# Attention with local band and global keys, then Fourier mixing and a two-layer block: global keys in small blocks of the array, and rows 4 and 5 read backwards

## The chip, the cores and the metric

The kernel runs on one core of a Trainium2 chip. A core has five engines with a queue each: TensorE (PE, matrix products out of SBUF into PSUM banks), VectorE (DVE), ScalarE (ACT), GpSimd (POOL, which here issues most loads) and SyncE (SP, which issues transfers). An engine runs its own queue in order; semaphores tie the queues together. The metric is the device time of one execution in microseconds (us), median over runs.

TensorE multiplies a stationary operand that has been loaded into its array (the weights) with a moving one that is streamed through. The array can be used whole, written 128\*128 (rows \* columns), or as smaller blocks such as 64\*64, 64\*128 or 128\*32, each with its own weights. The rows are the contracted side, the columns the partitions of the result. A `tile_position` names the corner of the block.

## What is computed

Four batches, eight heads, 768 positions, head size 64. Attention in which a query sees the 96 keys up to itself and the first eight keys of the sequence ("global" ones), with a bias by distance; for a global key outside the band the distance counts as 96.

```python
scores = scale * np.matmul(q, k.transpose(0, 1, 3, 2))
is_global = pos[None, :] < int(n_global)                 # 8
is_local = (rel >= 0) & (rel < int(n_local))             # 96
dist = np.where(is_global & ~is_local, float(n_local), np.abs(rel))
scores = scores - slopes[:, None, None] * dist
scores = np.where(is_global | is_local, scores, -1e9)
a = softmax(scores);  x = a @ v          # then heads side by side: x is (4, 768, 512)
mixed = np.real(fft(fft(x, axis=1), axis=2))
u = x + mixed
un = (u - mean(u)) / np.sqrt(var(u) + 1e-06)
out = u + np.maximum(un @ w_ch1, 0.0) @ w_ch2            # 512 -> 2048 -> 512
```

The mixed part has a symmetry: with x real, row s and column n of it equal row 768 - s and column 512 - n (both taken modulo their length).

## The kernel before

The whole kernel is one stream of instructions. Functions name units of work with their needs and costs, and a planner (`Plan`) walks through them with its own clock for each engine, and emits whichever can start first. Its costs, and small numbers in a table `BIAS` that favour or delay single units, set the order; nothing is decided while the kernel runs. There are four streams of TensorE units: MIX (Fourier mixing), ATT (attention), PH (first product of the two-layer block) and PG (second product).

**Attention**, by batch `b` and pair of heads `hp`. `load_qk` and `load_v` bring q, k and v in, through POOL's queue; only the first pair's q and k come as 32-bit through SP (L426) and are cast by an engine (L443). `trans` transposes q and k on TensorE (L507), or, from batch 2, a transfer does it (L485). `score` makes local scores: 64\*64 blocks in batches 0 and 1 (L549 adds the bias as a product, L559), 64\*128 blocks later (L555); ScalarE's exponential follows (L583 or L580). A 128-row block of queries has two blocks of keys, its own and the one before.

Global keys have a path of their own. `kg_copies` puts each head's eight global keys into a 32-column tile `kG`, in which every head has its own eight columns and the others hold zeros. `glob` makes scores of four heads at a time in a 128\*32 block (L639): the two products of a half add up, since each fills only its heads' rows. `v_global` gathers the eight heads' global values by a selecting product (L606) into `vG`, 64 rows (eight per head) by head; in the columns of head h all rows but h's eight are zero. A column of ones, made once by `ones` (L1423), gives the softmax its denominator. One exponential makes `EG` (L652).

`av` multiplies: for each of six blocks of queries it adds, in one place of a PSUM bank, the local products of both heads (L685, 65 columns: 64 values and the ones) and, from the third block on, one product of `EG` with both heads' part of `vG`, 130 columns (L677). Both use the whole array. VectorE divides by the denominator (L702, L704).

**Mixing.** In batches 1 to 3 `bounce` writes x to memory and reads it back with six sequence positions a partition (`XD`, `XR`), all through ScalarE's queue (L725, L732). `fold_s` and `fold_d` (VectorE) and `y_unit` (L914) make a transform of which only half is computed; the rest is the same data mirrored. `mirror` makes reversed copies on POOL: `r0` for rows 0 and 3 (L949 to L951), `rn` for the others (L962). `u_unit` makes u for a pair of rows (positions 6m + r) in one PSUM bank: the pairs are (1, 2), (0, 3), (4, 5), 16 products of 128 columns each (L1017). In batch 0 x is added into the bank by permuting products in 64\*64 blocks (L993, `spread`), in the others VectorE adds `XR` (L1039). Then comes the centring (L1073 and L1075), a transpose (`nt_unit`, L1114) and the sum of squares (L1082), with POOL's power (L1089, L1090).

**Two-layer block.** `ph_unit` (L1144) makes hidden units, ScalarE or VectorE applies the threshold (L1150, L1151), `pg_unit` (L1168) multiplies with the second weights, VectorE scales and adds u (L1177), SP stores (L1182). The last four of the twelve pairs of rows use a form with fewer products (L1249).

The planner charges 0.1 us where a unit marked narrow follows one that is not; the units of `av` are not marked.

Of the kernel before, what the change touches and what calls it, by code (L numbers as in the profile page):

```python
# [22 lines left out]
class Plan:  # L23
# [11 lines left out]
    def __init__(self):  # L35
        self.t = {"PE": 0.0, "ACT": 0.0, "DVE": 0.0, "POOL": 0.0, "SP": 0.7, "DMA": 3.75, "DMA2": 1.9}
        self.tok = {}
        self.ready = []
        self.pending = []
        self.rings = {}  # L40
        self.left = {}
        self.n = 0
        self.lanes = [0.0] * 8
        self.soft = [0.0] * 8
# [64 lines left out]
    def emit(self, place):  # L109
# [8 lines left out]
        if dma:  # L118
            q = "DMA2" if outs and outs[0] in (("ld", 0), ("ld", 1), ("c", "id"), ("c", "dist"), ("c", "gb")) else "DMA"
# [29 lines left out]
    def slot(self, tag):  # L149
# [7 lines left out]
    BIAS = {('mk1', '*', 4): 1.5, ('y', 1, 2, 2, 'r'): -3, ('qk', '*', 2): -0.7, (2, 90): -0.7, ('ob', '*', 2): -0.3,  # L157
            (3, '*', 7): -1.5, ('ex', 2, 2, 0): 1.5, ('ss', '*', 6): 0.3, (0, 20): -3, (1, 57): -0.7, ('mk1', '*', 5): 1.5,
            ('v', '*', 1): 1.5, ('c', 't2'): -0.3, ('mk1', '*', 7): 0.7, ('kG', '*', 1): 0.7, ('z', 1, 0): 3, ('u', 2, 0): 0.7}
# [4 lines left out]
    AQ = (4, 5)  # L164
    ORD = {("qk", 0): 0, ("v", 0): 0, ("qk", 1): 5, "w1": 6, "gate": 7, ("v", 1): 8, "w2": 9, ("qk", 2): 10, ("v", 2): 10, ("qk", 3): 10, ("v", 3): 10}
# [42 lines left out]
def act(n):  # L208
    return 0.06 + n / 1200.0


def dve(n):
    return 0.085 + n / 960.0
# [11 lines left out]
def kernel(  # L225
# [63 lines left out]
    sel = np.zeros((P, 128))  # L289
    gpos = np.flatnonzero(tau < NG)  # L290
    for h in range(4):
        for g in range(NG):
            sel[gpos[g], h * 32 + h * NG + g] = 1.0
    gb = np.zeros((64, 1))
    for h in range(H):
        at = 32 * (h // 2 % 2) + 16 * (h // 4) + 8 * (h % 2)
        gb[at:at + NG, 0] = -slopes[h] * NL
    perm = np.zeros((P, 9, 64))
    for rho in range(3):
        for jj in range(3):  # L300
            for m in range(64):
                y = 3 * m + rho - 64 * jj
                if 0 <= y < 64:
                    perm[y, 3 * rho + jj, m] = perm[64 + y, 3 * rho + jj, m] = 1.0
    ident_sel = np.concatenate([np.eye(P), sel], 1)
# [45 lines left out]
    ident = kon.tile([P, 256], FP16, tag="ident", name="ident")  # L351
    sel_sb = ident[:, 128:256]
# [4 lines left out]
    gb_sb = kon.tile([64, 1], FP32, tag="gb", name="gb")  # L357
# [7 lines left out]
    one = kon.tile([P, 1], FP16, tag="one", name="one")  # L365
# [3 lines left out]
    vG = [kon.tile([P, H, 66], FP16, tag=f"vG{i}", name=f"vG{i}") for i in range(2)]  # L369

    EG = kon.tile([P, 512], FP16, tag="eg", name="eg")
# [32 lines left out]
    def load_qk(b, hp):  # L404
# [3 lines left out]
        for w, src in enumerate((q, k)):  # L408
# [14 lines left out]
            if n == 0:  # L423
                def read(w=w, rows=rows):
                    t = stage["u", w] = buf("u", w, [P, 2 * NP, 2 * Dh], FP32, 1)
                    nc.sync.dma_start(t, rows)  # L426
                pl.later([("SP", 0.45, read)], [], 0.0, [("ld", w)], lat=1.7, dma=1.35)

                def cast(on, w=w):
                    place()  # L430
                    copy_on(on, qk16[n][:, w].rearrange("p h n t d -> p (h n) (t d)"), stage["u", w])
                pl.later([("ACT", act(768), lambda cast=cast: cast("ACT")), ("DVE", dve(768), lambda cast=cast: cast("DVE"))], [("ld", w)], 0.0,
                         [("qk", 0, w)], [("free", "u", w)], rank=0)
# [34 lines left out]
    def kg_copies(b, hp):  # L468
        n = HP * b + hp
        for s in range(2):  # L470
            def cp(on, s=s):
                c0 = 16 * (hp // 2) + 8 * s
                on.tensor_copy(  # L473
                    kG[b % 2][64 * s:64 * s + 64, hp, c0:c0 + NG].rearrange("p (t m) -> p t m", t=2),
                    TT[n][64 * s:64 * s + 64, 1, 0:P].rearrange("p (t m) -> p t m", t=2)[:, :, 0:NG // 2])
# [1083 lines left out]
```

## Time and profile before

The median of three runs is 263.35 us (262.07 to 263.92). The profiled execution took 262.43 us, its span from the first to the last instruction is 260.5 us. Durations are from that execution.

| what | instructions | busy us | mean ns of one |
|---|---|---|---|
| ph, first product (L1144) | 768 | 93.3 | 273 |
| pg, second product (L1168) | 256 | 61.1 | 379 |
| local attention products (L685) | 352 | 16.9 | 193 |
| global attention products (L677) | 64 | 12.6 | 220 |
| mixing, u (L1017), from plain tiles | 112 | 8.5 | 219 |
| adding x in batch 0 (L993) | 36 | 4.6 | 622 |
| global scores (L639) | 16 | 3.4 | 383 |
| reversed copies on POOL (L962) | 16 | 10.1 | 661 |
| VectorE's add of x to u (L1039) | 18 | 11.7 | 688 |
| exponential of global scores (L652) | 5 | 3.4 | 677 |

A row of the profile names the line, the engine, what is written and read, and the size as partitions x elements. Matmuls overlap, so their lengths add up to more than the busy time, and the price of one in a stream is the distance from its start to that of the next.

### The profile page before, as it was taken

How to read it: one execution, taken by the hardware profiler on the slowest of the kernel's cores; microseconds unless marked ns; L12 is line 12 of the kernel's file. 1: busy time of each engine (PE TensorE's matmuls, PEld its weight loads, DVE VectorE, ACT ScalarE, POOL GpSimd, SP SyncE). 2: the span in 40 equal slices, each digit the busy share in tenths (PEclk: the TensorE clock that was granted, in tenths of full speed). 3: DMA queues.
4: the chain of work that ended last, by engine and by line, in shares of the span. 5: the costliest groups of instructions: out<-in, count | busy, mean ns of one | idle time of the engine just before them, and what ended most of it. 6: DMA issues, size and time to landing. Idle time of an engine off the chain costs nothing.

```text
span 260.5 us, 6774 instructions
## 1 busy us (share of the span) xinstructions
PE 246.3 (95%) x2824; PEld 178.8 (69%) x2824; DVE 163.1 (63%) x362; ACT 142.9 (55%) x240; POOL 120.6 (46%) x212
## 2 busy tenths in 40 slices
PE   7798789899979999999999999999999999999994
PEld 2566545589748676575477466588779578888883
DVE  1549996537982746712277987778996555625463
ACT  4198798685636698851055743884645236533300
POOL 8798876724938988999921304030304011010000
PEclk9799999999999999999999999999999999999999
DMA  7999999997999999999968941401450540300222
GB/s 175 174 165 179 274 207 108 90 194 102 138 159 218 158 138 149 140 112 123 114 126 167 178 182 48 115 3 43 108 178 0 83 121 0 93 30 3 81 83 81
DMA packets 93630, 31.52 MB, mean 121 GB/s; under 512 B 81664, under 2 KB 89984, under 8 KB 93600
## 3 DMA queue, kind: packets, MB, share of 16 engines
q0 software_dynamic: 66096, 14.18, 62.5%
q1 hardware_dynamic: 24672, 12.19, 21.2%
q10 hardware_dynamic: 2832, 4.72, 6.9%
q8 instruction: 22, 0.36, 0.6%
q14 instruction: 8, 0.07, 0.1%
HBM read 30.95 MB, written 8.65 MB: 152 GB/s over the span
## 4 chain that ended last, share of the span: by engine, by line
PE 55%; POOL 19%; DMA 17%; ACT 3%; DVE 3%; issue 2%; ACTq 0%; POOLq 0%
PE ph L1144 18%; PE pg L1168 12%; POOL qk L414 10%; DMA v<-in_v_dram 7%; DMA qk<-in_q_dram 6%; PE pgD L1249 5%; POOL v L400 5%; DMA w<-in_moe_w_ch_dram 4%; PE pgA L1249 4%; PE pav L685 3%; PE py L914 3%; PE pu L1017 2%; PE pt L507 1%; DVE x L704 1%; POOL hT L438 1%
## 5 line engine op out<-in xcount | busy, mean ns | idle before, releaser
L1144 PE MATMUL ph<-unT,w 128*128 128x256 f16 x768 | 93.3, 273 | 2.9 <-ACT hT L1150 1.7
L1144 PEld LDWEIGHTS <-w 128*128 128x128 f16 x768 | 73.1, 98 | 16.1 <-issue 4.9
L1150 ACT ACTIVATE hT<-ph 128x512 f16<-128x512 f32 x83 | 48.9, 596 | 47.6 <-PE ph L1144 47.3
L1168 PE MATMUL pg<-w,hT 128*128 128x512 f16 x256 | 61.1, 379 | 0.0
L1168 PEld LDWEIGHTS <-hT 128*128 128x128 f16 x256 | 24.1, 98 | 23.8 <-issue 1.2
L1089 POOL TENSOR_SCALAR sm<-sm 128x2 f32<-128x2 f32 x12 | 3.0, 254 | 57.4 <-ACT un L1082 57.2
L400 POOL DMA_DIRECT2D v<-in_v_dram x32 | 24.7, 823 | 0.7 <-DMA hT<-in_k_dram 0.7
L583 ACT ACTIVATE ex<-sc 128x992 f16<-128x992 f32 (+2 forms) x24 | 20.6, 928 | 7.1 <-DVE qkT L514 5.6
L580 ACT ACTIVATE er<-sc 128x768 f16<-128x768 f32 (+2 forms) x24 | 21.6, 925 | 4.5 <-PE sc L555 3.3
L414 POOL DMA_DIRECT2D qk<-in_k_dram x32 | 21.4, 750 | 4.6 <-DMA qk<-in_k_dram 3.1
L1177 DVE SCALAR_TENSOR_TENSOR u<-pg,sm,u 128x512 f32<-128x512 f32 x16 | 12.0, 750 | 18.0 <-PE pg L1168 18.0
L414 POOL DMA_DIRECT2D qk<-in_q_dram x32 | 21.4, 730 | 3.4 <-DMA qk<-in_q_dram 2.0
L1073 ACT ACTIVATE un<-u,sm 128x512 f16<-128x512 f32 x17 | 11.8, 717 | 19.1 <-DVE sm L1043 17.6
L962 POOL COPY ww<-zy 128x512 f16<-128x512 f16 x16 | 10.1, 661 | 21.4 <-PE py L914 14.4
L595 DVE TENSOR_TENSOR ex<-er,mk 128x768 f16<-128x768 f16 (+2 forms) x24 | 15.4, 662 | 4.2 <-ACT er L580 4.2
L1082 ACT ACTIVATE un<-un 128x512 f16<-128x512 f16 x24 | 14.9, 625 | 4.5 <-DMA unT<-un 4.5
L1039 DVE SCALAR_TENSOR_TENSOR u<-pu,xr 128x512 f32<-128x512 f32 x18 | 11.7, 688 | 9.0 <-PE pu L1017 9.0
L685 PE MATMUL pav<-v,ex 128*128 128x65 f16 x352 | 16.9, 193 | 0.0
L473 POOL COPY kG<-qkT 64x8 f16<-64x8 f16 x28 | 9.6, 342 | 15.7 <-DMA qkT<-qk 12.8
L685 PEld LDWEIGHTS <-ex 128*128 128x128 f16 x352 | 15.6, 97 | 0.8 <-issue 0.2
L1151 DVE TENSOR_SCALAR hT<-ph 128x512 f16<-128x512 f32 x13 | 9.0, 690 | 8.3 <-PE ph L1144 8.3
L931 DVE CAST zy<-py 128x512 f16<-128x512 f32 (+1 forms) x8 | 7.1, 892 | 10.4 <-PE py L914 8.2
(143 smaller groups left out, 388.6 us busy)
## 6 DMA issues: line engine op xcount, KB each, us to landing
out_dram<-u SPq DMA_DIRECT2D x23, 256.0 KB, 2.1
w<-in_moe_w_ch_dram POOLq DMA_DIRECT2D x8, 512.0 KB, 11.0
v<-in_v_dram POOLq DMA_DIRECT2D x32, 96.0 KB, 6.5
xr<-xd ACTq DMA_DIRECT2D x3, 768.0 KB, 4.7
qk<-in_q_dram POOLq DMA_DIRECT2D x32, 48.0 KB, 4.0
qk<-in_k_dram POOLq DMA_DIRECT2D x32, 48.0 KB, 3.7
xd<-x ACTq DMA_DIRECT2D x4, 384.0 KB, 4.6
hT<-in_q_dram POOLq DMA_DIRECT2D x5, 192.0 KB, 7.4
```

The lines of the kernel that those rows point to most:

```text
L400: nc.gpsimd.dma_start(v16[b % 2][64 * t:64 * t + 64, h0:h0 + 2, :, 0:Dh].rearrange("m h i d -> m (h i) d"), v[b, h0:h0 + 2].rearrange("h ( ...
L414: nc.gpsimd.dma_start(qk16[n][64 * t:64 * t + 64, w, :, h], src[b, h0 + h].rearrange("(i m t) d -> t m i d", m=64, t=2)[t])
L580: A(mine(), cut(pa), AF.Exp, 0.0, 0.125)
L583: A(cut(expst[hp][:, :, g * 512:g * 512 + (384 if g == 2 else 512)]), cut(pa), AF.Exp, 0.0, 0.125)
L595: VT(o, mine(), m, op=ALU.mult)
L685: nc.tensor.matmul(o[:, s * 65:(s + 1) * 65], lhsT, v16[b % 2][:, 2 * hp + s, i, 0:65], start=(j < 2 and a == 0), stop=(a == len(ops) - 1) ...
L1082: A(x, x, AF.Square, accum_out=MV[c][:, a, 2:3])
L1144: nc.tensor.matmul(ph[:, a * CH:(a + 1) * CH].rearrange("p (x m) -> p x m", x=2), W1[0][:, d, jb * P:(jb + 1) * P], UNT[c][:, :, d, :], st ...
L1150: pl.later([("ACT", act(512), lambda: A(dst, ph, AF.Relu)), ("DVE", dve(512), lambda: V.tensor_scalar_max(dst, ph, 0.0))], [], e, [("h", c ...
L1168: nc.tensor.matmul(pg, HT[c][:, jb, t * P:(t + 1) * P], W2[0][:, jb, :], start=(jb == 0), stop=(jb == NJ - 1))
L1177: V.scalar_tensor_tensor(UT[c][:, t, :], pg, MV[c][:, t, 3:4], UT[c][:, t, :], op0=ALU.mult, op1=ALU.add)
L1249: nc.tensor.matmul(o, lhs(j), rhs(j), start=(first and j == 0), stop=(j == NK - 1), skip_group_check=True)
```

## The change

**Global keys.** Each pair of heads now has its own group of 32 rows (`HQ` gives the place), with sixteen rows of it for one half of the positions and sixteen for the other, of which four each are global keys and the rest get a bias of -30000, so their exponential is zero. `kG` is one copy per pair instead of two, without the zeros. `glob` makes a product per head in a 64\*32 block, `EG` holds both heads of a pair beside each other, with an exponential for each. `v_global` is one product per pair, which brings the ones along. `av` has a global product per head, with 32 rows of weights.

**Rows 4 and 5.** The pairs are (1, 2), (4, 5), (0, 3). In batch 0 rows 4 and 5 are made in reverse order of their positions from the plain tiles; in the others they have no product, and VectorE reads the bank of rows 1 and 2 backwards in both directions. Their part of `XR` comes by an indirect transfer with reversed indices, and their result is stored by one, both through POOL. `rn` goes. The re-read of x moves from ScalarE's queue to SP's. In batch 0 the spread's loops run in the other order on both sides.

**Start and order.** The identity is loaded ahead of k, pair 2's q and k of batch 0 come through SP too, nine warming products replace twelve, `ones` goes, some zero fills go, one fold step of batch 0 may go to either engine, several of the planner's costs are changed, and `BIAS` is a new table, so that the order of units changes throughout.

```diff
 def kg_copies(b, hp):
-        for s in range(2):
-            def cp(on, s=s):
-                c0 = 16 * (hp // 2) + 8 * s
-                on.tensor_copy(kG[b % 2][64 * s:64 * s + 64, hp, c0:c0 + NG]..., TT[n][64 * s:64 * s + 64, 1, 0:P]...[:, :, 0:NG // 2])
+        def cp(on):
+            on.tensor_copy(kG[b % 2][:, hp, :].rearrange("p (t m) -> p t m", t=2),
+                           TT[n][:, 1, 0:P].rearrange("p (t m) -> p t m", t=2)[:, :, 0:16])
 def v_global(b, halves):
-                for h in range(4):
-                    nc.tensor.matmul(pv[32 * half:32 * half + 32, 0, h * 64:(h + 1) * 64], sel_sb[:, h * 32:(h + 1) * 32],
-                                     v16[b % 2][:, 4 * (h // 2) + 2 * half + h % 2, 0, 0:Dh], ..., tile_position=(0, 32 * half))
+                for hp in (half, half + 2):
+                    o = 32 * HQ[hp]
+                    nc.tensor.matmul(pv[o:o + 32, 0, 0:130]..., sel_sb, v16[b % 2][:, 2 * hp:2 * hp + 2, 0, 0:65],
+                                     start=True, stop=True, tile_position=(0, o))
 def glob(b, halves):
-                    nc.tensor.matmul(pg[32 * half:32 * half + 32, 0, :], kG[b % 2][:, hp, :], TT[HP * b + hp][:, 0, 256:S],
-                                     start=(i == 0), stop=(i == 1), tile_position=(0, 32 * half))
+                for s in range(2):
+                    r, o = slice(64 * s, 64 * s + 64), 32 * HQ[n % HP]
+                    nc.tensor.matmul(pg[o:o + 32, s, :], kG[b % 2][r, n % HP, :], TT[n][r, 0, 256:S],
+                                     start=True, stop=True, tile_position=(64 * s, o))
-                A(EG[rows], pg[rows, 0, :], AF.Exp, gb_sb[rows], 0.125)
+                for s in range(2):
+                    A(EG[rows, s], pg[rows, s, :], AF.Exp, gb_sb[rows, s:s + 1], 0.125)
 def av(b, hp):
-                    if j >= 2:
-                        nc.tensor.matmul(o..., EG[:, (j - 2) * P:(j - 1) * P], vG[b % 2][:, 2 * hp:2 * hp + 2, 0:65],
-                                         start=True, stop=False, skip_group_check=True)
                     for s in range(2):
+                        if j >= 2:
+                            r = slice(32 * HQ[hp], 32 * HQ[hp] + 32)
+                            nc.tensor.matmul(o[:, s * 65:(s + 1) * 65], EG[r, s, (j - 2) * P:(j - 1) * P], vG[b % 2][r, s, 0:65],
+                                             start=True, stop=False, skip_group_check=True, tile_position=(32 * HQ[hp], 0))
                         ops = [(expst[hp][:, s, j * 256:j * 256 + P], j)]
 def bounce(b):
-            eng.dma_start(XR[b], rows)
+            nc.sync.dma_start(XR[b][:, 0:4], rows[:, 0:4])
+        def rg():
+            nc.gpsimd.indirect_dma_start(out=XR[b][:, 4:6]..., in_=XD[b]..., in_offset=bass.IndirectOffsetOnAxis(ap=back_sb[:, 0:1], axis=0))
+        pl.later([("POOL", 1.2, rg)], [("xw", b), ("xr", b), ("c", "back")], 0.0, [("xg", b)], lat=2.2, dma=0.8, rank=0)
 def spread(pu):
-    nc.tensor.matmul(pu[64 * h:64 * h + 64, a, :].rearrange("p (r n) -> p r n", r=4), PX[0][t, ...], X[0][t, 3 * h + jj].rearrange("p (n r) -> p r n", r=4), ...)
+    hx = 1 - h if pr == 1 else h
+    nc.tensor.matmul(pu[64 * h:64 * h + 64, a, :].rearrange("p (r n) -> p n r", r=4), PX[0][t, ...], X[0][t, 3 * hx + jj].rearrange("p (n r) -> p n r", r=4), ...)
+def evac(c, pu, ring, e, pr):        # batches 1 to 3; called for rows 1 and 2, and for 4 and 5 on the same bank
+        def back():
+            for a in range(2):
+                o, x = (t[:, i].rearrange("p (n r) -> p r n", r=4) for t, i in ((u, a), (XR[b], 4 + a)))
+                i = pu[:, 1 - a, ::-1].rearrange("p (r n) -> p r n", r=4)
+                V.scalar_tensor_tensor(o[:, 1:4], i[:, 0:3], 1.0, x[:, 1:4], op0=ALU.mult, op1=ALU.add, accum_out=sm[:, a, 0:1])
+                V.scalar_tensor_tensor(o[:, 0, 1:P], i[:, 3, 0:P - 1], 1.0, x[:, 0, 1:P], op0=ALU.mult, op1=ALU.add, accum_out=sm[:, a, 4:5])
+                V.tensor_tensor(u[:, a, 0:1], pu[:, 1 - a, 0:1], XR[b][:, 4 + a, 0:1], op=ALU.add)
+            V.tensor_tensor(sm[:, :, 0], sm[:, :, 0], sm[:, :, 4], op=ALU.add)
+            V.tensor_tensor(sm[:, :, 0], sm[:, :, 0], u[:, :, 0], op=ALU.add)
+            V.tensor_scalar_mul(sm[:, :, 1], sm[:, :, 0], -SC / Dm)
+def store_back(c, needs):
+            nc.gpsimd.indirect_dma_start(out=out.rearrange("b (n r) d -> (b n) (r d)", r=2),
+                                         out_offset=bass.IndirectOffsetOnAxis(ap=back_sb[:, b:b + 1], axis=0),
+                                         in_=UT[c].rearrange("p r d -> p (r d)"), in_offset=None)
...
-        for _ in range(12):
+        for _ in range(9):
```

## The prediction

> **What bounds the kernel now.** I read the page's busy shares by slice first, then busy time by stretch, then the order of TensorE's work, then its matmuls by shape, then the waits.
>
> ```profile
> PE 246.3 (95%) x2824; PEld 178.8 (69%) x2824; DVE 163.1 (63%) x362; ACT 142.9 (55%) x240; POOL 120.6 (46%) x212
> PE   7798789899979999999999999999999999999994
> DVE  1549996537982746712277987778996555625463
> PEclk9799999999999999999999999999999999999999
> ```
>
> TensorE (PE) is 95% busy and from the thirteenth of the forty slices (78 us) to the last but one stands at nine tenths or more, at full clock. What lengthens its queue there lengthens the span; what other engines gain or lose there does not, unless PE then waits.
>
> ```profile
> core 0: us, PE busy (x) PEld busy (x) DVE busy (x) ACT busy (x) POOL busy (x), PEclk, DMA share, GB/s
> 17.00:30.00 13.00, 11.65 (x307) 9.03 (x296) 10.57 (x34) 11.36 (x17) 10.80 (x18) 1.00 1.81 215
> 30.00:47.00 17.00, 14.96 (x234) 8.96 (x232) 13.38 (x40) 13.97 (x22) 12.26 (x23) 1.00 1.19 153
> 60.00:130.00 70.00, 67.90 (x646) 46.29 (x642) 37.61 (x72) 39.12 (x66) 59.70 (x98) 1.00 1.54 141
> 130.00:200.00 70.00, 69.80 (x760) 50.76 (x759) 56.41 (x113) 41.66 (x70) 14.36 (x31) 1.00 0.45 107
> ```
>
> Batch 0's attention and mixing (17 to 47 us) is the one place where four engines are all near full and PE has gaps: 30.0 - 26.6 = 3.4 us idle. From 60 to 200 us it idles 2.3 us in 140.
>
> ```profile
> 139.07 0.22 PE L677 MATMUL pav<-vG,eg 128*128 128x130 f16 x1
> 139.13 0.28 PE L685 MATMUL pav<-v,ex 128*128 128x65 f16 x4
> 139.25 0.22 PE L677 MATMUL pav<-vG,eg 128*128 128x130 f16 x1
> ...
> 139.76 1.92 PE L1144 MATMUL ph<-unT,w 128*128 128x256 f16 x16
> 141.52 1.03 PE L1168 MATMUL pg<-w,hT 128*128 128x512 f16 x4
> 142.48 0.59 PE L555 MATMUL sc<-qkT 64*128 64x256 f16 x8
> 143.00 1.92 PE L1144 MATMUL ph<-unT,w 128*128 128x256 f16 x16
> 144.85 0.83 PE L555 MATMUL sc<-qkT 64*128 64x256 f16 x8
> ```
>
> Columns: start, length, engine, line, tiles, block of the array used (rows*columns), size. Length includes a pipelined tail, so a matmul's price is the distance between starts. Two facts. Inside attention x values (pav) one global matmul of 130 columns and four local ones of 65 take 0.18 us, 57 + 4 x 29 ns: the price of a matmul is its columns at 0.42 ns, and loading its weights is hidden. And a change of block shape costs. Sixteen ph matmuls followed by the same 128*128 shape take 141.52 - 139.76 = 1.76 us; the same sixteen followed by a 64*128 block take 144.85 - 143.00 = 1.85 us. Taken from the start of each single matmul, less the columns before it, all 15 changes from 64*128 to 128*128 cost 95 to 96 ns each and 15 of the 16 the other way 98 or 99; those to and from 128*32, 128*64 and 64*64 mostly cost 92 to 99, and more only after a wait or after blocks that did not run side by side. The kernel makes 80 of them.
>
> ```profile
> L685 PE MATMUL pav<-v,ex 128*128 128x65 f16 x352 | 16.9, 193 | 0.0
> L677 PE MATMUL pav<-vG,eg 128*128 128x130 f16 x64 | 12.6, 220 | 0.0
> ```
> ```profile
> PE ph L1144 <- ACT hT L1150: 1.7, 1, 1.7
> ```
> ```profile
> ACT mk L1407 <- DMA xd<-hT: 4.0, 1, 4.0
> ```
>
> The last two belong together: near 76 us ScalarE (ACT) holds the issue of batch 1's re-read of xd in its queue, sits 4.0 us until the write lands, and PE, short of hidden units, loses 1.7 us.
>
> **The global values' product, the term that decides.** All 64 matmuls of L677 used the full 128*128 block, like the local ones around them. They become 128 matmuls of 32 rows (32*128), one per head, each set between 128*128 matmuls in the same accumulation. Columns: 64 x 57 = 3.6 us before, 128 x 29 = 3.7 after, nothing. But each is entered and left by a change of shape: 256 new changes (in the built order the total goes from 80 to 338). No 32-row block is in the trace; the nearest rows are the 64-row ones, 98 ns in and 95 out. 128 x (98 + 95) = 24.7 us, 6.2 in each batch. Below, the bound is 0 (the array might keep its mode for fewer rows); above, nothing over 99 was seen without a wait. I take the row.
>
> Of this, batches 1 to 3, 18.5 us, lie in a queue with next to no gaps: all of it on the path. In batch 0, 6.2 us meet 3.4 us of gaps, so 2.8 to 6.2 count; the gaps are partly waits on VectorE (DVE) work that itself follows these products, so I let them hide only 2.0: +4.2.
>
> The Trainium skill, TensorEngine Tiling, Key Properties, says that a change of tiling mode drains the array, and TensorE: Matmul & The Clock Gate, in its step-by-step section, that a drain is about 128 cycles. By an estimate from that page, 53 ns a change at the column rate above, the two terms would be 10.3 and 1.4 us and the total would land near 268. The 95 ns of the rows decide.
>
> **Other edits on PE.** Rows 4 and 5 of batches 1 to 3 no longer have their own mixing product: VectorE reads rows 1 and 2 backwards out of the same bank. 3 x 16 matmuls of 128 columns, 0.89 us a group in the chain of waits: -2.7. Global scores: four 512-column matmuls on two 128*32 blocks go pairwise, 0.44 us a batch; eight on eight separate 64*32 blocks should go at once, 0.22. Batch 0's two calls save as much each: five times 0.22, -1.1 (0 if the eight share what feeds them, as no row shows). The spread of x over batch 0's u (L993) sends 512 columns in 0.43 us for four blocks where the score blocks of the same shape send 496 in 0.23; it now reads x contiguously and writes the bank strided. Nine groups: -2.0 if the strided read was the cause, 0 if the strided write costs the same, and as much as +2.0 if it costs double; I take -1.0, nearer to the contiguous row. Gathering the values (vG) and the ones: tenths of a us either way.
>
> **The wait at 76 us.** The re-read of xd moves to SyncE's (SP) queue, so ScalarE no longer holds its exponentials and hidden units behind it: -1.7. Behind the wait on SP now stand stores and the transposes of batch 2's q and k; their users come tens of us later. What is late next on ScalarE is nothing: it has 39 of 70 us busy. If those transposes are late, up to 1.7 comes back.
>
> **DVE, ACT, POOL, DMA.** VectorE's backward add is split into 384, 127 and 1 columns for two rows and three small sums. From rows of the same kind (512: 688 ns, 128: 288) a 384 comes to 550, 127 to 288, one element to 150, plus 84 to read an accumulator each: 2 x 1.16 + 3 x 0.16 = 2.8 us against 1.7, +1.1 in three batches. It lies under PE work (VectorE 56 of 70 us busy in the fullest stretch); without that cover it is +3.3. Global exponentials: two of 0.68 instead of one, five times, 3.4 us, under ScalarE's 55%. GpSimd (POOL) loses sixteen reversals (10.1 us) that PE hardly waited for (0.2 us), and issues three gathers and four scattered stores through its queue; no row shows such a DMA. The nearest are its loads, 0.73 to 0.87 us to issue and 4 to 7 to land; 7 x 0.8 = 5.6 us, less than what it sheds. A gather waits for the re-read, and the loads of q and k behind it on POOL wait with it.
>
> **Head.** Identity is loaded second, not third, and q and k of pair 2 come through SP with casts on ScalarE. PE waited 2.1 us for the identity, so 0 to -2.1; pair 2, now 768 KB behind k and the distances, may give it back: -0.5.
>
> **Sum.** +18.5 + 4.2 - 2.7 - 1.1 - 1.7 - 1.0 - 0.5 = +15.7. The profiled execution took 262.43 us (span 260.5 and 1.9 around it), 0.9 under the median of 263.35. 262.43 + 15.7 = 278.1, against the median's level **279.0**.
>
> **Rivals.**
> 1. *A 32-row block beside full blocks changes no mode.* Then the first two terms vanish and -7.0 is left: 255.4, or 256.3 at the median's level, faster. For it: no 32-row shape is in the trace. Against: every one of the seen pairs of shapes pays, row splits like column splits. It decides if the change in and out costs under 27 ns each (7.0 us / 256).
> 2. *Only one of the two changes costs*, or each half: 9.2 + 1.1 - 7.0 = +3.3, 267. For it: nothing but the different neighbour; against: 98 in and 95 out, both ways full.
> 3. *The backward path becomes a wait.* The rows of pair 2 need write, re-read, a gather of one more landing (4.7 us as the re-read's), then 2.8 us of VectorE: 7.5 us later than the first pair, where ph of the first pair covers 8 x 0.87 = 7 us and the second products of the pair before some more. If those have run out, and loads stuck behind a gather on POOL add to it, 2 to 3 us in each of three batches: +8, 287.
>
> **Chances.** As forecast, within some 6 us: 0.73. Rival 1: 0.07. Rival 2: 0.08. Rival 3: 0.12. The range 267 to 288 holds the main case with its open terms (batch 0's 2.8 to 6.2, the spread's 4, the head's 2, the scores' 1.1), rival 3's centre and the upper edge of rival 2; outside are rival 1, half of rival 2 and half of rival 3. About 1% either way, 260.7 to 266.0, can't be told from no change. Faster 0.07; same 0.04, the lower side of rival 2; slower 0.89.
>
> **What would show it.** In the profile after: a local matmul that follows a global one starts some 120 ns after it (27 of columns and 95), not 29; a pair's attention product takes 1.5 us longer; TensorE at nine tenths or more in the same slices, a longer span. ScalarE's 4.0 us wait gone; eight global score matmuls within 0.25 us of each other; spread groups at 0.22. I am wrong if global matmuls start 29 ns after their neighbours, or if TensorE shows new gaps of several us ahead of the second pair's hidden units.

## The result and the profile after

The changed kernel took 290.94 us (median of four runs, 288.33 to 291.64) against 262.76 us for the kernel before: a ratio of 1.104 (95% interval 1.098 to 1.110). The forecast was 279.0, with a range of 267 to 288. The sign was right; the time lies 12 us above the forecast and 3 us above the range. The profiled execution took 290.45 us, its span is 288.7.

From the page, TensorE's busy time, its share by slice, and its granted clock:

```profile
PE 275.0 (95%) x2829; PEld 192.7 (67%) x2829; DVE 167.2 (58%) x389; ACT 142.3 (49%) x234; POOL 112.1 (39%) x183
PE   6589998989999999999999999999999999999995
PEclk9577779999999999999959999999999999999999
```

TensorE is as full as before, 95%, with five matmuls more and 28.7 us more of busy time. No engine took its place and no gap opened: a stream of nearly the same matmuls is longer. The clock row has something new. It stood at nine in all slices but one before; now it dips in the second to sixth and again near 145 us.

Busy time by stretch (TensorE's matmuls first, its granted clock after the five engines); the last four rows are for the section on the clock:

```profile
core 0: us, PE busy (x) PEld busy (x) DVE busy (x) ACT busy (x) POOL busy (x), PEclk, DMA share, GB/s
17.00:30.00 13.00, 12.35 (x190) 8.01 (x190) 4.38 (x12) 6.74 (x9) 10.58 (x15) 0.76 1.85 205
30.00:47.00 17.00, 15.81 (x258) 10.12 (x252) 13.69 (x53) 11.78 (x16) 5.37 (x9) 0.83 1.26 172
60.00:130.00 70.00, 68.71 (x736) 49.26 (x728) 41.33 (x93) 38.77 (x69) 49.15 (x77) 1.00 1.35 137
130.00:200.00 70.00, 70.00 (x610) 43.26 (x608) 42.78 (x93) 35.89 (x58) 21.37 (x37) 0.95 0.65 100
...
20.00:25.40 5.40, 4.88 (x96) 3.36 (x93) 1.89 (x4) 4.75 (x7) 4.82 (x7) 1.00 1.83 179
25.44:32.26 6.82, 6.82 (x71) 3.63 (x72) 2.93 (x10) 2.11 (x3) 4.83 (x7) 0.50 1.44 266
141.50:144.90 3.40, 3.40 (x43) 2.42 (x41) 0.62 (x2) 0.09 (x1) 3.40 (x6) 1.00 1.91 183
144.90:148.30 3.40, 3.40 (x26) 2.24 (x25) 2.18 (x6) 0.00 (x0) 0.27 (x1) 0.50 1.53 190
```

Between 130 and 200 us 760 matmuls were done before and 610 are done now, with TensorE busy throughout. A busy share does not say how much is computed.

The timeline of TensorE (start, length, tiles, block, size):

```profile
54.54 1.48 PE L989 MATMUL pu<-x,er 64*64 64x512 f16 x12
...
59.74 0.41 PE L640 MATMUL pgl<-qkT,kG 64*32 64x512 f16 x8
60.08 0.40 PE L556 MATMUL sc<-dist,sid 64*64 64x480 f16 x4
...
142.96 0.24 PE L686 MATMUL pav<-v,ex 128*128 128x65 f16 x2
143.12 0.20 PE L679 MATMUL pav<-vG,eg 32*128 32x65 f16 x1
143.26 0.23 PE L686 MATMUL pav<-v,ex 128*128 128x65 f16 x2
143.42 0.20 PE L679 MATMUL pav<-vG,eg 32*128 32x65 f16 x1
...
145.30 0.23 PE L679 MATMUL pav<-vG,eg 32*128 32x65 f16 x1
145.46 0.29 PE L686 MATMUL pav<-v,ex 128*128 128x65 f16 x2
145.69 0.23 PE L679 MATMUL pav<-vG,eg 32*128 32x65 f16 x1
```

One global product and two local ones repeat every 0.30 us (143.12 to 143.42). Their columns are 3 x 27 = 81 ns; nearly all of the other 0.22 us is the array changing shape twice. Taken from the starts of single matmuls, less their columns, the way in from a local product has a median of 102 ns (119 changes) and the way out of 104 ns (128 changes): 206 ns for each global product, where the forecast had 98 + 95 = 193. At half clock (145.30 to 145.69) the period is 0.39 us: the columns double to 162 ns, the rest stays near 0.23 us.

The groups of attention products show the same as a sum; before, they stood at 16.9 and 12.6 us:

```profile
L686 PE MATMUL pav<-v,ex 128*128 128x65 f16 x352 | 35.8, 203 | 0.0
L679 PE MATMUL pav<-vG,eg 32*128 32x65 f16 x128 | 25.9, 203 | 0.1
```

The waits of TensorE (total, times, longest) have changed too:

```profile
PE pt L514 <- ACT hT L452: 4.9, 2, 3.4
PE sc L556 <- ACT eg L652: 1.3, 2, 0.9
PE pz L1427 <- DVE eg L1422: 1.2, 1, 1.2
```

The 1.7 us for hidden units is gone, and so is ScalarE's 4.0 us for the write of x. New is a wait of 4.9 us for casts of q and k. The timeline of ScalarE at the start shows them (in brackets: idle before, and what ended it):

```profile
8.14 0.84 ACT L452 ACTIVATE hT<-u 128x768 f16<-128x768 f32 x1 [3.49 <-DMA u<-in_k_dram]
11.99 0.84 ACT L452 ACTIVATE hT<-u 128x768 f16<-128x768 f32 x1 [3.00 <-DMA u<-in_q_dram]
14.35 0.84 ACT L452 ACTIVATE hT<-u 128x768 f16<-128x768 f32 x1 [1.51 <-DMA u<-in_k_dram]
15.09 1.84 ACT L590 ACTIVATE ex<-sc 128x992 f16<-128x992 f32 x2
```

The first pair's k, cast at 5.77 us before, is now cast at 8.14. Pair 2's casts (11.99 and 14.35) stand in ScalarE's queue ahead of the first exponential, which now starts at 15.09 us (12.18 before). The first attention product starts at 22.8 us (18.7 before), the first hidden unit at 62.0 (50.6).

### The profile page after: what moved, and what is told of

Read it like the earlier page. It is cut to its first block, busy times and chain, and to the rows that moved or that the text cites. A ratio compares the mean times of both kernels' runs of the same rounds, so it can differ in the third digit from the quotient of the medians.

```text
span 288.7 us, 6768 instructions
## 1 busy us (share of the span) xinstructions
PE 275.0 (95%) x2829; PEld 192.7 (67%) x2829; DVE 167.2 (58%) x389; ACT 142.3 (49%) x234; POOL 112.1 (39%) x183
## 4 chain that ended last, share of the span: by engine, by line
PE 78%; DMA 8%; ACT 4%; POOL 4%; DVE 3%; SPq 1%; issue 1%; POOLq 0%; ACTq 0%; DVEq 0%
PE ph L1169 25%; PE pg L1202 16%; PE pav L686 9%; PE pav L679 6%; PE pgD L1286 5%; DMA u<-in_k_dram 4%; PE pgA L1286 4%; PE py L924 3%; ACT ex L590 3%; DMA out_dram<-u,back 3%; PE pu L1014 2%; PE pt L514 2%; DMA v<-in_v_dram 2%; POOL qk L423 2%; PE sc L562 2%; POOL v L409 2%
## 5 line engine op out<-in xcount | busy, mean ns | idle before, releaser
L1169 PE MATMUL ph<-unT,w 128*128 128x256 f16 x768 | 95.3, 276 | 0.3 <-DVE hT L1176 0.2
L686 PE MATMUL pav<-v,ex 128*128 128x65 f16 x352 | 35.8, 203 | 0.0
L587 ACT ACTIVATE er<-sc 128x992 f16<-128x992 f32 (+2 forms) x24 | 21.7, 928 | 12.2 <-DVE ex L602 7.8
L679 PE MATMUL pav<-vG,eg 32*128 32x65 f16 x128 | 25.9, 203 | 0.1
L703 DVE RECIPROCAL rc<-pav 128x12 f32<-128x12 f32 (+1 forms) x20 | 4.3, 216 | 34.9 <-PE pav L686 34.9
L686 PEld LDWEIGHTS <-ex 128*128 128x128 f16 x352 | 19.1, 99 | 6.5 <-issue 0.2
L602 DVE TENSOR_TENSOR ex<-er,mk 128x992 f16<-128x992 f16 (+2 forms) x24 | 14.7, 625 | 5.2 <-ACT er L587 5.0
L679 PEld LDWEIGHTS <-eg 32*128 32x128 f16 x128 | 11.7, 92 | 8.9 <-issue 1.9
L1186 POOL DMA_INDIRECT out_dram<-u,back x4 | 4.2, 1050 | 33.0 <-DVE u L1211 19.0
L736 POOL DMA_INDIRECT xr<-xd,back x3 | 3.6, 1200 | 30.5 <-DVE zy L783 19.9
```

Of the source, the lines that this page charges most:

```text
L587: A(mine(), cut(pa), AF.Exp, 0.0, 0.125)
L602: VT(o, mine(), m, op=ALU.mult)
L679: nc.tensor.matmul(o[:, s * 65:(s + 1) * 65], EG[r, s, (j - 2) * P:(j - 1) * P], vG[b % 2][r, s, 0:65], start=True, stop=False, skip_group ...
L686: nc.tensor.matmul(o[:, s * 65:(s + 1) * 65], lhsT, v16[b % 2][:, 2 * hp + s, i, 0:65], start=(j < 2 and a == 0), stop=(a == len(ops) - 1) ...
L1169: nc.tensor.matmul(ph[:, a * CH:(a + 1) * CH].rearrange("p (x m) -> p x m", x=2), W1[0][:, d, jb * P:(jb + 1) * P], UNT[c][:, :, d, :], st ...
```

## The experiments

The theory: a 32-row product between full ones pays two changes of shape, and these 256 changes are nearly the whole loss. Rivals: fewer rows in themselves, or twice as many products and weight loads, are what costs; or the rest of the change (rows 4 and 5, the start, the new order) costs and the array does not.

| kernel | what differs | us | ratio to the kernel before (95%) |
|---|---|---|---|
| b_rows32 | before, global product on 32 rows, 64 of them | 273.11 | 1.036 (1.027 to 1.045) |
| b_rows32_heads | before, on 32 rows by head, 128 | 288.69 | 1.096 (1.086 to 1.105) |
| b_heads | before, on 128 rows by head, 128 | 263.66 | 1.002 (0.998 to 1.005) |
| a_full | after, on 128 rows by head | 261.69 | 0.993 (0.990 to 0.997) |
| a_grouped | after, on 32 rows, in groups | 266.01 | 1.011 (1.002 to 1.020) |
| a_head | after, old start | 292.82 | 1.115 (1.108 to 1.122) |
| a_full_head | a_full, old start | 258.24 | 0.983 (0.980 to 0.985) |
| a_full_hw0 | a_full, only the old loads | 259.49 | 0.985 (0.978 to 0.993) |
| a_full_id | a_full, only the old identity and warming | 263.85 | 1.004 (1.000 to 1.008) |
| a_rows45 | after, old global path and old start | 261.61 | 0.996 (0.993 to 0.999) |

Differences below are taken from the kernel before as run in the same group: 263.41 us for b_rows32, b_rows32_heads, a_full and a_grouped, 263.11 for a_head, a_full_head, b_heads and a_rows45, 263.34 for a_full_hw0 and a_full_id.

**Rows, products, changes: three edits of the kernel before.** Pairs that share a half have zeros in each other's columns, and the other half's 32 rows are all zeros for a pair, so 32 rows give the same sum.

```diff
 # b_rows32
-  matmul(o..., EG[:, (j - 2) * P:(j - 1) * P], vG[b % 2][:, 2 * hp:2 * hp + 2, 0:65], ...)
+  r = slice(32 * (hp % 2), 32 * (hp % 2) + 32)
+  matmul(o..., EG[r, (j - 2) * P:(j - 1) * P], vG[b % 2][r, 2 * hp:2 * hp + 2, 0:65], ..., tile_position=(32 * (hp % 2), 0))
```

> The kernel before, with one edit: the 64 products of the global values (L677) read only the 32 rows that hold their pair's keys, as 32*128 blocks, so 128 changes of block shape are added and nothing else moves. Theory 1, a change of shape costs what the profile after shows (102 ns in, 104 out) and nothing more: 128 x 0.103 = 13.2 us, less up to 2 in batch 0's gaps: ratio 1.04 to 1.05, clock as before. Theory 2, the drained stretches also lose the granted clock: half clock in one or more windows of 3.4 or 6.8 us inside the attention products, each costing half its length, 1.055 to 1.075. Rival, a 32-row block is free and the loss after came from the new order and the head: 0.995 to 1.005.

```diff
 # b_rows32_heads: inside "for s in range(2)", ahead of head s's local products
+  matmul(o[:, s * 65:(s + 1) * 65], EG[r, (j - 2) * P:(j - 1) * P], vG[b % 2][r, 2 * hp + s, 0:65], ..., tile_position=(32 * (hp % 2), 0))
```

> The kernel before, with the product of the global values as the changed kernel has it: one per head, 32*128 blocks, each between local products, 256 changes of shape added. Theory 1, shape changes alone: 256 x 0.103 = 26.4 us less some 2: ratio 1.09 to 1.095, granted clock as before. Theory 2, clock lost as well: 1.11 to 1.14, with half-clock windows in the attention products. Rival, order and head: 0.995 to 1.005.

```diff
 # b_heads: as b_rows32_heads, on all 128 rows
+  matmul(o[:, s * 65:(s + 1) * 65], EG[:, (j - 2) * P:(j - 1) * P], vG[b % 2][:, 2 * hp + s, 0:65], ...)
```

> The kernel before with the global product per head, but on all 128 rows: 64 more matmuls, 128 of 65 columns for 64 of 130, no change of shape. Control for b_rows32_heads. Theory 1: 64 more matmuls at 2 ns each, ratio 0.997 to 1.003, no half clock past the start. Rival, the number of matmuls and weight loads matters (64 loads of some 53 ns): 1.01 to 1.015.

Measured: +9.7, +25.3 and +0.6 us, ratios of 1.036, 1.096 and 1.002. The control came as expected; the first is a little under the range for shape changes alone, the second a little over it and under the range with a lost clock. Sixty-four more products and weight loads cost nothing that can be told from no change; 32 rows instead of 128 cost 9.7 us with 128 changes and 25.3 with 256. The timeline of b_rows32 gives the price where nothing else was changed:

```profile
143.38 0.23 PE L678 MATMUL pav<-vG,eg 32*128 32x130 f16 x1
143.54 0.29 PE L686 MATMUL pav<-v,ex 128*128 128x65 f16 x4
143.76 0.23 PE L678 MATMUL pav<-vG,eg 32*128 32x130 f16 x1
```

A group of one and four takes 0.38 us where it took 0.18 before: 0.20 us for two changes, medians of 97 and 105 ns. 128 changes at 101 ns are 12.9 us, 3 us more than the time shows. TensorE idles 2.8 us less after its first attention product than in the kernel before (7.4 against 10.2 us; the 1.7 us wait for hidden units is gone), so gaps took up most of that. The second kernel is more than twice as dear as the first, which the count of changes alone does not give. The granted clock by slice on the page of b_rows32 is full but for the start:

```profile
PEclk9599999999999999999999999999999999999999
```

On the page of b_rows32_heads it dips three times past the start, each time at attention products:

```profile
PEclk9796769999999999999998999999999999999999
```

On the page of b_heads, with the same products on all 128 rows, it is full past the start, as in the kernel before. Over the runs, the mean granted clock of an execution is 0.964 to 0.970 in b_rows32_heads and 0.981 to 1.000 in b_heads.

**The changed kernel with 128 rows, and in groups.** In a_full each pair's part of vG has zeros outside its 32 rows, and `av` reads all 128, head by head: the same count of matmuls, no change of shape.

```diff
 # a_full
-  vG = [kon.tile([P, 2, 66], ...)]
+  vG = [kon.tile([P, H, 66], ...)]        # zeroed once; each pair's 32 rows are copied to its own two heads
-  matmul(o[:, s * 65:(s + 1) * 65], EG[r, s, (j - 2) * P:(j - 1) * P], vG[b % 2][r, s, 0:65], ..., tile_position=(32 * HQ[hp], 0))
+  matmul(o[:, s * 65:(s + 1) * 65], EG[:, s, (j - 2) * P:(j - 1) * P], vG[b % 2][:, 2 * hp + s, 0:65], ...)
```

> The changed kernel with one edit: the product per head of the global values uses all 128 rows, with zeros in the values' tile for the other pairs (four copies a batch instead of one), so the 256 changes of shape go and the number and columns of the products stay. Theory 1, shape changes alone, the clock lost to the slower head: 291 - 26 = 263 to 266, the half-clock windows at 25, 39 and 145 us still there. Theory 2, the clock goes with the drains: those windows vanish as well, 17.1 us at half clock are worth 8.5, 254 to 258. Rival, order and head are the loss: 287 to 291.

```diff
 # a_grouped: all global products of three blocks ahead of the local ones, so one change in and one out for each group
+  for j in range(max(2, 3 * x), 3 * x + 3):
+      for s in range(2):
+          at = (j - 3 * x) * 130 + s * 65
+          matmul(po[:, x, at:at + 65], EG[r, s, ...], vG[b % 2][r, s, 0:65], ..., tile_position=(32 * HQ[hp], 0))
```

> The changed kernel with one edit: in each attention unit the 32-row products of the global values come first, side by side, and the local ones after them, so a unit makes two changes of shape instead of up to twelve: 64 of 256 are left. Theory 1: 192 x 0.103 = 19.8 us less: 270 to 273, clock windows as after. Theory 2: the stretches are dense again and the clock comes back: 260 to 266. Rival: 287 to 291.

In a_grouped part of the global keys' contribution is missing from the output; the matmuls are all there. Measured: a_full is 29.25 us below the changed kernel, and 1.7 below the kernel before. a_grouped, with 64 changes, is 4.3 us above a_full, at the upper end of theory 2; 64 x 103 ns would be 6.6, and its clock is full past 20 us. So 32 rows by themselves are not what costs. The timeline of TensorE in a_full has a local product start 0.03 us after the global one:

```profile
129.65 0.19 PE L681 MATMUL pav<-vG,eg 128*128 128x65 f16 x1
129.68 0.22 PE L688 MATMUL pav<-v,ex 128*128 128x65 f16 x2
129.74 0.19 PE L681 MATMUL pav<-vG,eg 128*128 128x65 f16 x1
```

From one global product to the next: 0.09 us here, 0.30 in the changed kernel, with the same columns. The half-clock stretches at 25, 39 and 145 us are gone with the changes, as theory 2 had it (the mean clock is 0.979 to 1.000 over its runs, 0.947 to 0.958 in the changed kernel), while 261.69 us lies between the ranges of the two theories. The granted clock of a_full:

```profile
PEclk9779999999999999999999999999999999999999
```

Busy time from the first attention product to the first hidden unit and from there to the end, two rows of the changed kernel and two of a_full:

```profile
22.83:62.02 39.19, 36.27 (x558) 23.32 (x551) 25.79 (x86) 24.10 (x35) 17.50 (x29) 0.87 1.12 145
62.02:288.66 226.64, 223.05 (x2067) 160.18 (x2060) 134.95 (x280) 106.91 (x187) 78.41 (x128) 0.98 0.69 98
...
23.68:55.86 32.18, 26.68 (x550) 18.01 (x550) 25.97 (x88) 23.84 (x35) 17.48 (x29) 1.00 1.34 171
55.86:260.63 204.77, 200.75 (x2067) 149.34 (x2060) 135.63 (x286) 107.70 (x190) 80.38 (x128) 1.00 0.77 109
```

Together the changed kernel takes 28.9 us longer here: TensorE is busy 31.9 us more and idles 3.0 us less. Of the 31.9, 256 x 103 ns = 26.4 are changes. That leaves 5.5 for the lower clock and for what else differs between the two orders. An estimate of the clock alone agrees: the columns that the changed kernel streams in its half-clock stretches (25.4 to 32.3, 39.1 to 42.5 and 144.9 to 151.7 us) take 12.6 us there, and would take half of that, 6.3 us less, at full clock. Both parts bear this out: before the first hidden unit 64 changes (6.6 us) and the clock (3.8 by that estimate) stand against 9.6 us more of busy time and 2.6 less of idling; after it 192 changes (19.8) and the clock (2.5) against 22.3 more and 0.4 less.

**The start.** The old start means: only the first pair's q and k through SP with casts (`HW = (0,)`, `U0 = 2`), q, k and then the identity, twelve warming products.

```diff
 # a_head, a_full_head: all of it; a_full_hw0: the first two lines; a_full_id: the others
-    HW = (0, 2)
-    U0 = 4
+    HW = (0,)
+    U0 = 2
...
-        dma_const(ident, id_d, 0.3, ("c", "id"))     # ahead of k
+        dma_const(ident, id_d, 0.3, ("c", "id"))     # behind k
-        for _ in range(9):
+        for _ in range(12):
```

> The changed kernel with its 32-row global products kept and only the start of the kernel before put back. Theory 1, start and drains add: 291 less some 5: 284 to 287. Rival, drains hide the late start: 290 to 292. If the half-clock windows inside the attention products are due to the late start, they vanish here; if to the drains, they stay.

> The changed kernel with full-row global products (as in a_full) and the start of the kernel before: q, k, then the identity; only pair 0 through SP; twelve warming products. The planner makes a new order from it. In a_full the first hidden unit (ph) began at 55.9 us against 50.6 before, and the end was level. Theory 1, the new start alone costs those 5 us and they reach the end: 256 to 258.5. Rival, the late start is made up by work that is ready anyway: 260.5 to 262.5.

> The kernel with the global values' product on all 128 rows (261.69 us, first hidden unit at 55.9 us, first values' product at 23.7), with one part of the old start back: only the first pair's q and k come through SP and are cast, pair 2's again through POOL's queue. With the whole old start back the kernel took 258.24, first hidden unit 51.8. Theory A: the start lost because pair 2's 768 KB shared the transfers with the first pair's k, and its casts stood on ScalarE ahead of others; then this alone gets nearly everything: 258.2 to 259.3, first values' product by 20.5 us. Rival B: the identity, ahead of k on SP, and the shorter warming lost it; then this stays at 261 to 262, first values' product at 23.

> The same kernel with the other part of the old start back: q, k, then the identity, and twelve warming products, while pair 2's q and k still come through SP with casts on ScalarE. Theory A: little changes, 261 to 262.3, first values' product at 23 us. Rival B: 258.2 to 259.3, first values' product by 20.5 us. If both runs gain about 1.7 us, each part has half.

With full rows the old start gains 3.45 us (258.24 against 261.69), the upper edge of theory 1. The loads alone gain 2.2 (259.49, a little over theory A's range), so pair 2's loads and casts are what the new start pays for. The order of the identity and the warming, put back alone, lose 2.2, which neither theory had. The two parts don't add up: with the old loads, putting the identity back as well gained a further 1.25, but the intervals of those two kernels overlap. ScalarE's timelines show what is late, first in a_full_head, then in a_full_hw0 (old loads only), then in a_full_id (old identity only):

```profile
4.16 0.84 ACT L452 ACTIVATE hT<-u 128x768 f16<-128x768 f32 x1 [2.15 <-DMA u<-in_q_dram]
5.29 0.84 ACT L452 ACTIVATE hT<-u 128x768 f16<-128x768 f32 x1 [0.28 <-DMA u<-in_k_dram]
10.82 2.56 ACT L590 ACTIVATE ex<-sc 128x992 f16<-128x992 f32 x3 [4.69 <-PE sc L566]
...
8.18 0.84 ACT L452 ACTIVATE hT<-u 128x768 f16<-128x768 f32 x1 [3.35 <-DMA u<-in_k_dram]
11.66 2.56 ACT L590 ACTIVATE ex<-sc 128x992 f16<-128x992 f32 x3 [2.64 <-PE sc L566]
...
5.00 0.84 ACT L452 ACTIVATE hT<-u 128x768 f16<-128x768 f32 x1 [0.28 <-DMA u<-in_k_dram]
14.49 0.84 ACT L452 ACTIVATE hT<-u 128x768 f16<-128x768 f32 x1 [1.44 <-DMA u<-in_k_dram]
15.24 2.54 ACT L590 ACTIVATE ex<-sc 128x992 f16<-128x992 f32 x3
```

The first pair's k is cast late (8.2) where the identity goes out ahead of it, whether pair 2 follows on SP or not, and early (5.0 and 5.3) where it doesn't. The first exponential is late (15.2) where pair 2's casts stand in front of it, even with an early k, and not where they don't (10.8 and 11.7). So it is the casts, standing in the queue until pair 2's loads land, that hold the exponentials up, and not a transfer of k slowed by pair 2's 768 KB. As to a_full_id's loss: TensorE idles more than half of the stretch from 30.6 us, 1.9 us of it waiting for VectorE, and half clock follows, which a_full doesn't have there:

```profile
30.58:33.99 3.41, 1.46 (x50) 1.37 (x47) 2.50 (x14) 1.45 (x1) 2.88 (x5) 1.00 1.19 234
33.99:37.40 3.41, 3.41 (x60) 2.64 (x60) 2.54 (x9) 1.22 (x1) 0.67 (x2) 0.50 1.25 203
```

How much of the 2.2 us that explains was not tried. a_full_hw0 has one such stretch too, from 52.5 us.

a_full_head is faster than both kernels of this study: 0.983 of the kernel before.

In a_head, where the 32-row products stay, the same start gained nothing: 292.82 us, against 290.94, above both ranges; the half-clock stretches inside the attention products stayed, so the late start is not their cause. The first attention product did start earlier (20.0 against 22.8 us). But a shift of the start reorders what follows, and its busy time by stretch shows a loss that the changed kernel does not have:

```profile
192.70:196.80 4.10, 4.10 (x51) 2.90 (x48) 1.41 (x4) 0.75 (x2) 0.00 (x0) 1.00 0.00 0
196.80:203.60 6.80, 6.80 (x42) 4.80 (x41) 2.11 (x5) 1.36 (x3) 0.00 (x0) 0.50 0.19 42
...
207.04:213.87 6.83, 6.83 (x37) 4.18 (x38) 3.79 (x7) 1.80 (x4) 0.00 (x0) 0.50 0.00 0
```

Two stretches of 6.8 us at half clock in batch 3, where the changed kernel kept the full clock. In all, a_head runs 30.7 us at half clock past its first attention product, the changed kernel 17.1; by the same estimate from columns that is 12.6 us lost against 6.3.

**Rows 4 and 5 alone.** a_rows45 is the changed kernel with the old `kg_copies`, `v_global`, `glob`, `ones` and 130-column products of `av` put back, and the old start: what remains is rows 4 and 5, the re-read of x on SP, the spread's loops and the new order.

```diff
 # a_rows45, in av (the other functions likewise as in the kernel before)
+  if j >= 2:
+      matmul(o..., EG[:, (j - 2) * P:(j - 1) * P], vG[b % 2][:, 2 * hp:2 * hp + 2, 0:65], ...)
-  matmul(o[:, s * 65:(s + 1) * 65], EG[r, s, ...], vG[b % 2][r, s, 0:65], ..., tile_position=(32 * HQ[hp], 0))
```

> The changed kernel with the whole path of the global keys as before (scores by four heads with zeros, values with zeros, the ones) and with the start of before: what is left is rows 4 and 5 read backwards, the re-read through SP, the spread's order and a new planner's order. Theory 1: three mixing products less and the wait on the hidden units gone, 2.7 + 1.7: 257.5 to 260. Rival, the gathers and the longer backward add give it back: 262 to 264. Against a_full_head it shows what the new global path is worth without its drains: 1.1 by the scores' blocks.

Measured: 261.61, 1.5 us faster than before, less than expected and between the two ranges. Its first hidden unit starts at 53.1 us, 2.5 later than before, and TensorE's waits have new entries, from the order that the planner makes:

```profile
PE pgD L1296 <- DVE mk L1278: 1.2, 1, 1.2
PE ph L1179 <- ACT ex L594: 1.0, 1, 1.0
```

So part of what rows 4 and 5 save may be given back in this order; that was not tried by itself. a_full_head, which differs from it in the global path, is 3.4 us faster. The forecast gave the global scores 1.1; what the other 2.3 us are was not tried apart.

## Why the prediction was off

**Right: the price of a change of shape, the sign, and TensorE's queue as the bound.** What makes the global values' product dear is the change of shape, not columns, rows or weights: b_heads with its 64 extra products costs nothing, a_grouped keeps the 32 rows and loses most of the cost, a_full without changes takes the loss away. Rival 1 (no change of mode) and rival 2 (half of the changes cost) fall by the 102 and 104 ns. Rival 3 (the backward path) did not happen: TensorE's list of waits has no entry on it. VectorE's backward rows were dearer than forecast, 853 ns for 384 elements and 384 for 127 (550 and 288 had been taken), and stayed hidden.

The signs that were promised: a local product starts 0.14 us after the global one (143.12, 143.26; promised 0.12); a pair's product is longer by 8 x 206 ns = 1.65 us, worked out from the changes (promised 1.5); the stretch at nine tenths is as full as before; ScalarE's 4.0 us is gone; eight global score products end in 0.34 us, 0.24 without the change of shape that follows, as promised. The spread was not as promised.

The forecast was 11.9 us low. By its own terms:

| term of the sum | forecast us | measured us | short by |
|---|---|---|---|
| global values' product, batches 1 to 3 and batch 0 | 18.5 + 4.2 | 256 x 103 ns = 26.4, less 3.0 taken up by idle time | 0.7 |
| granted clock | none | 31.9 - 26.4 = 5.5, other differences of order in it | 5.5 |
| head | -0.5 | 261.69 - 258.24 = 3.45, with full rows | 3.9 |
| spread of x | -1.0 | 1.48 us for 12 products, 1.53 before, three times: -0.1 | 0.9 |

That is 11.0 of the 11.9. The row on the head holds along this path, with the 32-row products taken out first; with them in place the old start gained nothing (a_head).

**First failed step: no term for the clock.** The forecast reckoned with a clock that had stood at nine in 39 of 40 slices, "at full clock", and priced a longer queue at that clock. The 32-row products lowered it: 17.1 us at half clock past the first attention product, none in a_full, and the same between b_rows32_heads and b_heads. That is 5.5 us by the traces, the largest part of the miss, and no term and no end of the range stood for it.

**Second: the head.** It was weighed (identity earlier, pair 2 "may give it back") and set at -0.5, bounded by 0 to -2.1; the wrong bound was above. Two casts more wait in ScalarE's queue in front of the first exponential, which the step did not count: it starts at 14.7 to 15.7 us in the four kernels with these casts in front (the changed one, a_full, a_full_id, a_grouped), at 10.8 to 12.9 in the eight others. And the identity ahead of k, which the step took for a gain, has k cast some 3 us later (8.18 in a_full_hw0, 5.29 in a_full_head).

**Third: the spread.** Writing the bank with a stride costs nearly what reading x with a stride had cost (1.48 and 1.53 us); the end of 0 was in the range.

**Nearly right: the term that decides.** "I take the row" gave 193 ns from the 64-row rows; a 32-row block beside a full one costs 206, so "nothing over 99" was no upper bound, which is 1.7 us in all. "I let them hide only 2.0" was near as well: 2.6 us in batch 0, 3.0 in the whole. The smaller estimate, 53 ns a change by the Trainium skill (TensorE: Matmul & The Clock Gate, step-by-step section), is half of the 102 and 104 ns measured; the choice of the row over it was right.

The remaining terms (rows 4 and 5, global scores, the wait at 76 us) came to -5.5. With full rows and the old start all of them together gave 258.24 - 263.11 = -4.9. So their sum was near; a_rows45, 1.5 us under the kernel before, did not reach what rows 4 and 5 and the wait were to give in the order that the planner made for it.

## What to carry to other kernels

Price a small block set among others by its changes of shape: here 206 ns for a matmul whose columns are 27 ns, while filling the same product up with zero rows to the full array cost nothing. If a small block is needed, put blocks of one shape together (64 changes instead of 256 took 25 of the 29 us away). And look at the clock: a stretch that is full of such changes can be followed by half clock, which then lengthens what comes next. Work added ahead of the first scores, here two casts before the first exponential, can be paid at the start however idle the engine is on average: 3.45 us with full rows.

## What was not expected of the hardware

**Changes of shape can lower the clock while TensorE reads as busy.** From 141.5 to 144.9 us the changed kernel's TensorE is busy 3.40 of 3.40 us, and at 144.9 the granted clock drops to 0.50 (last rows of the windows above). From the matmul records and the granted clock of the traces:

```
stretch of attention products only     half clock from (for)
after            22.8 us, 6.1 long      25.4 (6.8)
after            33.6 us, 5.1 long      39.1 (3.4)
after           141.5 us, 5.6 long     144.9 (6.8)
a_head           20.0 us, 3.3 long      26.1 (3.4)
a_head           29.4 us, 5.6 long      33.0 (6.8)
a_head          138.2 us, 5.4 long     142.2 (6.8)
a_head          192.7 us, 5.4 long     196.8 (6.8)
a_head          203.2 us, 5.7 long     207.0 (6.8)
b_rows32_heads   19.4 us, 3.3 long      24.1 (6.8)
b_rows32_heads   29.7 us, 5.7 long      34.3 (6.8)
b_rows32_heads  145.6 us, 5.2 long     150.3 (3.4)
b_rows32         27.3 and 136.7, 3.4    none
```

In the first three kernels 81 of 300 ns stream columns, 27%; in b_rows32 162 of 375, 43%. Every stretch at 27% of 3.3 us or more was followed by half clock; none of the stretches up to 2.6 us was, between which hidden units stand.

The twelve traces say more. In each of them the granted clock changes only at steps of 3.41 us, counted from its first change. Cut the traces into these windows and add up, from the starts of the matmuls, the time in which columns stream (0.42 ns a column, 0.83 at half clock):

```
windows at full clock, by share of streaming    followed by half clock
0.39 and under                                  28 of 29
0.40 to 0.45                                     1 of 7
0.46 and over                                    0 of 838
windows at half clock                           followed by full clock
under 0.75                                       0 of 14
0.75 to 0.79                                     3 of 6
0.80 and over                                   23 of 23
```

The one at 0.39 or under that kept its clock is the last whole window of its trace. TensorE's busy share doesn't part them: ten of the 29 have TensorE busy in 0.87 to 1.00 of the window, all full of 32-row changes, while windows busy in 0.50 to 0.60 of it, with 0.44 and more streaming, kept full clock. The half clock in a_full_id (34.0 us) and a_full_hw0 (52.5), with no 32-row product in them, fits too: 0.34 and 0.37 of the windows before stream. So, by these windows, the changes of shape lower the clock as waiting does, by taking time from streaming. This is read from twelve profiled executions; no kernel was built to try it, for instance by parting the long stretches alone. The Trainium skill (TensorE: Matmul & The Clock Gate, the section HAM oscillation) puts the loss of clock down to gaps of over some 3.4 us in which TensorE idles; these stretches have no gap, so here the windows decide.

**The price of a change hardly follows the clock.** The two changes take 0.21 us together at full clock and 0.23 at half (medians of 101 and 104 ns against 121 and 109), while the columns take twice as long.

**VectorE reading a bank backwards with a stride** took 853 ns for 384 elements, where 512 read forwards take 687.
